# Induced attention and gated network on one core: one planner setting for all stretches, an earlier second softmax, reciprocals by a bit guess and three Newton steps

## The chip, the cores and the metric

The kernel runs on one core of one Trainium2 chip. The metric is the device time of one launch in microseconds (us); three runs of the kernel before gave 713.29, 713.41 and 719.63 us, median 713.41. Engines are named as in the profile: PE (matrix products), PEld (its weight loads), DVE (VectorE), ACT (ScalarE), POOL (GpSimd) and SP (the queue that issues most transfers).

## The reference

```python
def mab(q, kv):                      # x: 4 x 12416 x 128, inducing: 32 x 128
    s = scale * (q @ kv.transpose(0, 2, 1))
    s = s - s.max(-1, keepdims=True)
    a = np.exp(s)
    a /= a.sum(-1, keepdims=True) + 1e-09
    return a @ kv
h = mab(I, x)                        # first softmax: 32 rows over 12416 tokens
y = mab(x, h)                        # second softmax: each token over 32 rows
gate = 1.0 / (1.0 + np.exp(-(y @ w_gate)))          # 128 -> 1536
out = gate * (y @ w_val) @ w_out                    # 1536 -> 128
```

## The kernel before

Each of the four batches has 97 groups of 128 tokens. The second softmax is not applied to h: the kernel multiplies h by the two weight matrices once per batch (`hw`, two parts of 12 x 128 columns), so that a token's 32 attention weights, spread four times over the 128 partitions and transposed by a DMA (`a2r`), give gate and value directly. The main loop works on 97 **blocks**, 96 of 512 tokens of one batch and a last one of four times 128 tokens, one piece from each batch. Each block has 12 **chunks** j of 128 hidden columns. For a chunk PE fills 512 columns of gate and of value in PSUM (`emit_fill`, L1172 to L1190), ACT takes tanh(gate / 2) into `t16` (`emit_gate`, L1192), DVE makes u = (t + 1) * value in one SCALAR_TENSOR_TENSOR (`emit_product`, L1206), and PE multiplies the four quarters of u with `wo16` and adds them up in the block's output bank (`emit_out`, L1222 to L1238: four **output products** to a chunk). After 12 chunks ACT moves the bank out, times 0.5 (`emit_evict`, L1248), and SP stores it.

Chunks go through in **steps** of two and one in turn: PSUM has one bank pair (two-chunk) and one bank (one-chunk) for gate and the same for value. So the value fill of a step must wait until the product of the step of its own size ahead of it has read the bank, and the gate fill until that step's tanh has. There are three `t16` buffers and `UBUFS = 5` u buffers for each size: a product writes the buffer of the fifth product of its size ahead of it, and has to wait until that one's output products are done.

An **aside** is a chunk that DVE doesn't work on. PE fills its gate and value in a side bank (L1557), ACT takes the tanh (L1567), POOL adds 1 (L1571), ACT copies the value out of PSUM (L1575), and POOL multiplies (L1578). Its four output products belong to the same block as the others, and a block's bank is moved out after its last output product, asides included.

Beside this loop run, for later blocks: the second softmax in groups of 16 x 128 tokens (`op_stage2`: scores on PE, copy by ACT L474, row maximum by a tree on POOL L484 to L492, exponential on ACT L502, sums by a tree on POOL L510, reciprocals on POOL `s2_inverse_pool` L532, spread on POOL L562, transposing DMA on SP L573), and the first softmax of the next batch (`op_stage1`; its group sums are 28 to 32 small PE matmuls into `hp_ps`, L356).

The order of all this on every engine is made when the kernel is built, by a planner in the kernel: it keeps a time for each engine and, for each operation, a cost and a time to its result, and takes at each point what is ready. `TIMES` says from which place (batch, chunk of four blocks) an operation of the softmaxes may start: "late" gives the starts of the second softmax's groups 2 to 5. `SETTINGS` are thresholds of the planner, one row for each stretch of eight blocks; rows only name what differs from the row before. Among them: `most` asides in a block, `lead` (an aside is begun only where the next product lies at least so many planned ns behind ACT), `eager` (how far an eviction may push a tanh), `guard` (PE work in the last 3413 planned ns below which PE gets a matmul with zeros, a **pulse**, L1745). Engines run their queues in the planned order; the planned times themselves are not used on the chip, where semaphores decide.

## Time and profile before

| | |
|---|---|
| median of 3 runs | 713.41 us |
| the profiled execution's own time | 713.61 us |
| its span, first to last instruction | 711.7 us |
| busy in the span: PE, DVE, ACT, POOL | 695.2, 696.7, 676.5, 477.6 us |
| first product begins, last one ends | 30.46, 707.13 us |
| products on DVE, asides on POOL | 762 steps (1143 chunks), 21 |

A group's row of the profile has the line of the kernel, engine, operation, the tile written and the tiles read, the shapes and how often; then busy time of the group in us and mean ns of one instruction; then idle time ahead of it and what ended it. Durations of neighbouring instructions on one engine overlap a little, so that the busy time of a group (without the overlap) is less than count times mean. A row of a timeline has the start and how long it took in us, and neighbours of one kind are merged (x3). The row of a window has, for each engine, the busy us and the instructions, then the granted clock of TensorE.

### The profile page before, as it was taken

What the parts mean: (1) busy time and instruction counts of PE and PEld (TensorE: products, weight loads), DVE (VectorE), ACT (ScalarE), POOL (GpSimd) and SP (SyncE); (2) the same over time, 40 slices, a digit from 0 to 9 for tenths busy, and PEclk for the clock granted to TensorE, in tenths of its full rate; (3) what the DMA queues carried; (4) which work ended last, traced back from release to release, by engine and by line L of the source; (5) the groups of instructions that cost most, each with busy time, mean ns of one, the idle gap of its engine ahead of it and who ended that gap; (6) DMA issues with size and microseconds to landing.
All of it is one profiled execution on the core that took longest, in us unless ns stands there. A gap on an engine that the chain in (4) does not pass through costs nothing.

```text
span 711.7 us, 21558 instructions
## 1 busy us (share of the span) xinstructions
PE 695.2 (98%) x8449; PEld 409.0 (57%) x8449; DVE 696.7 (98%) x864; ACT 676.5 (95%) x1035; POOL 477.6 (67%) x743
## 2 busy tenths in 40 slices
PE   7999999999999999999999999999999999999997
PEld 4455555655555555655555555565565565565555
DVE  5899999999999999999999999999999999999997
ACT  4699999999999999999999999999999999999996
POOL 3587577868776874889865785678755688774221
PEclk9999999999999999999999999999999999999999
DMA  9795795324369534243448532302022022122011
GB/s 208 115 190 120 132 161 113 86 81 97 100 131 166 117 69 113 68 105 63 100 86 156 94 92 61 89 33 74 34 76 76 31 76 60 47 76 76 32 46 46
DMA packets 118181, 65.76 MB, mean 92 GB/s; under 512 B 101408, under 2 KB 102208, under 8 KB 118080
## 3 DMA queue, kind: packets, MB, share of 16 engines
q1 hardware_dynamic: 112176, 50.90, 31.2%
q0 software_dynamic: 5584, 13.34, 11.3%
q8 instruction: 66, 1.08, 0.6%
q14 instruction: 35, 0.29, 0.1%
q10 hardware_dynamic: 320, 0.15, 0.1%
HBM read 27.80 MB, written 25.43 MB: 75 GB/s over the span
## 4 chain that ended last, share of the span: by engine, by line
PE 79%; DVE 8%; ACT 7%; issue 2%; DMA 2%; POOL 1%; DVEq 0%; ACTq 0%; POOLq 0%
PE acc_ps L1231 39%; PE v_ps L1180 30%; DVE u L1206 7%; ACT t L1194 6%; PE g_ps L1180 5%; DMA xn<-in_x_dram 2%; PE s_ps L431 2%; PE hp_ps L356 1%; PE s_ps L296 1%; POOL xT L562 0%; ACT o L1248 0%; PE xt_ps L617 0%; PE side_g_ps L1557 0%; POOL hpart L660 0%; PE hw_ps L397 0%
## 5 line engine op out<-in xcount | busy, mean ns | idle before, releaser
L1206 DVE SCALAR_TENSOR_TENSOR u<-t,v_ps 128x1024 f16<-128x1024 f16 x763 | 664.8, 944 | 0.7 <-PE acc_ps L1231 0.3
L1194 ACT ACTIVATE t<-g_ps 128x1024 f16<-128x1024 f32 x762 | 583.2, 831 | 14.2 <-ACT t L1194 5.7
L1231 PE MATMUL acc_ps<-wo,u 128*128 128x128 f16 x4572 | 388.0, 221 | 1.9 <-ACT o L1248 1.6
L1231 PEld LDWEIGHTS <-u 128*128 128x128 f16 x4572 | 262.5, 98 | 165.3 <-issue 162.8
L1180 PE MATMUL v_ps<-a2r,hwt 32*128 32x512 f16 (+1 forms) x1167 | 291.8, 375 | 4.5 <-DVE u L1206 1.1
L1180 PE MATMUL g_ps<-a2r,hwt 32*128 32x512 f16 (+1 forms) x1167 | 290.4, 374 | 0.0
L1180 PEld LDWEIGHTS <-hwt 32*128 32x128 f16 x2358 | 106.0, 91 | 94.3 <-issue 10.7
L562 POOL TENSOR_TENSOR a2n<-e,rs 128x2048 f16<-128x2048 f16 (+1 forms) x23 | 83.9, 3648 | 1.8
L535 POOL TENSOR_TENSOR near<-sme,minus 128x16 f32<-128x16 f32 (+1 forms) x22 | 65.2, 2963 | 1.8
L1248 ACT ACTIVATE o<-acc_ps 128x512 f32<-128x512 f32 x96 | 58.4, 609 | 0.0
L486 POOL TENSOR_SCALAR rise<-rise 128x256 f32<-128x256 f32 (+6 forms) x110 | 51.0, 463 | 9.5
L1571 POOL TENSOR_SCALAR side_t<-side_t 128x512 f32<-128x512 f16 x21 | 31.4, 1496 | 30.3 <-ACT side_t L1567 30.2
L1578 POOL TENSOR_TENSOR side_t<-side_t,side_v 128x512 f16<-128x512 f32 x21 | 26.7, 1270 | 30.9 <-ACT side_v L1575 27.0
L484 POOL TENSOR_TENSOR rise<-sc 128x256 f32<-128x256 f32 (+1 forms) x22 | 16.2, 737 | 43.7 <-ACT sc L474 43.4
L510 POOL TENSOR_TENSOR sum<-e 128x256 f32<-128x256 f16 (+1 forms) x23 | 15.4, 670 | 44.3 <-ACT e L502 42.1
L510 POOL TENSOR_TENSOR sum<-sum 128x128 f32<-128x128 f32 (+3 forms) x92 | 28.3, 307 | 7.1
L488 POOL TENSOR_TENSOR top<-top,rise 128x128 f32<-128x128 f32 (+3 forms) x88 | 28.3, 322 | 6.8
L484 POOL TENSOR_TENSOR rise<-top 128x128 f32<-128x128 f32 (+3 forms) x88 | 27.2, 309 | 6.5
L492 POOL TENSOR_TENSOR sc<-sc,top 128x512 f32<-128x512 f32 (+1 forms) x22 | 23.9, 1085 | 1.7
L321 ACT ACTIVATE a1T<-s_ps,nm 128x512 f16<-128x512 f32 (+1 forms) x26 | 16.8, 646 | 3.3 <-DVE nm L308 3.2
L431 PEld LDWEIGHTS <-xT 128*128 128x128 f16 x388 | 14.2, 96 | 6.9 <-issue 6.4
L431 PE MATMUL s_ps<-hT,xT 128*128 128x32 f16 x388 | 17.9, 177 | 0.1
(157 smaller groups left out, 333.1 us busy)
## 6 DMA issues: line engine op xcount, KB each, us to landing
out_dram<-o SPq DMA_DIRECT2D x96, 256.0 KB, 2.1
xn<-in_x_dram POOLq DMA_DIRECT2D x18, 512.0 KB, 6.4
xn<-in_x_dram POOLq DMA_DIRECT2D x3, 544.0 KB, 6.2
xn<-in_x_dram POOLq DMA_DIRECT2D x3, 256.0 KB, 12.8
xn<-in_x_dram SPq DMA_DIRECT2D x1, 576.0 KB, 4.7
xn<-in_x_dram SPq DMA_DIRECT2D x1, 512.0 KB, 3.8
a2r<-a2n SPq DMA_TRANSPOSE x27, 4.3
wg<-in_moe_w_gate_dram POOLq DMA_DIRECT2D x1, 384.0 KB, 11.6
```

The source lines that it names most:

```text
L431: nc.tensor.matmul(s2[:, j, :], xT[b][:, c + j, :], hT16[b][:], start=(j == 0), stop=whole and j == j1 - 1, skip_group_check=True,)
L484: nc.gpsimd.tensor_tensor(out=r, in0=far, in1=near, op=ALU.subtract)
L486: nc.gpsimd.tensor_scalar_max(out=r, in0=r, scalar1=0.0)
L510: nc.gpsimd.tensor_tensor(out=d[:, 0:n, :], in0=src[:, :, 0:w], in1=src[:, :, w : 2 * w], op=ALU.add)
L535: nc.gpsimd.tensor_tensor(out=near[:, 0:n], in0=sme[:, 0:n], in1=minus1[:, 0:n], op=ALU.pow)
L562: eng.tensor_tensor(out=a2n[:, 0:n, :, :], in0=e.unsqueeze(2).to_broadcast((P, n, 4, m)), in1=rs.unsqueeze(2).unsqueeze(3).to_broadcast((P ...
L1180: nc.tensor.matmul(pt[:, k, col : col + nb * P], hw[b][r : r + 32, j // 2, :], a2r[r : r + 32, o : o + nb, :].rearrange("p j t -> p (j t)" ...
L1194: st["tanh"] = nc.scalar.activation(out=st["t"][:], in_=st["g"][:], func=AF.Tanh, scale=0.5)
L1206: u = nc.vector.scalar_tensor_tensor(out=st["u"][:, :, c:e], in0=st["t"][:, :, c:e], scalar=1.0, in1=st["v"][:, :, c:e], op0=ALU.add, op1= ...
L1231: nc.tensor.matmul(accs[i][(q // 2) % len(accs[i])][:, q, :], u[:, ts(q, P)], wo16[:, item["j"], :], start=begins, stop=last, skip_group_c ...
L1248: nc.scalar.mul(out=o32[:], in_=accs.pop(i)[0][:], mul=0.5)
L1571: nc.gpsimd.tensor_scalar_add(out=st["t1"][:], in0=st["t"][:], scalar1=1.0)
```

## The change

- One row of settings for all stretches, with `lead` 1900 (1500 or 1900 before), `most` 6 everywhere, and three new thresholds. `gap` is so large that it does nothing. With `rush`, an eviction may push a tanh by up to 2500 planned ns once 44 output products are queued. `ripe` halves the wait after which an aside's fill may go out of turn (4000 to 2000).
- The starts of the second softmax's groups move up by 0 to 6 places.
- Reciprocals: one power on POOL and a Newton step (4 instructions) become a bit guess by integer arithmetic and three Newton steps (10 instructions).
- The PE matmuls of a first softmax's group sum go out in one piece, not in two.
- In the last block, value and gate fills of a step are interleaved where both are ready.
- Pulses may begin earlier; the aside's sum has one buffer, not two; the zeros are set by DVE at the start. `HALVES` is off, `TBUFS` and `DEEP` keep the old numbers.

```diff
-    dict(most=6, warm=1500, margin=300, loose=150, lead=1500, calm=26, outq=40, quiet=1,
...
+    dict(most=6, warm=1500, margin=300, loose=150, lead=1900, calm=26, outq=40, quiet=1,
+        slack=90, guard=1800, hold=22, eager=300, keep=0, pace=9999, soft=80, push=36,
+        patience=6000, hurry=100, window=320, age=3500, ahead=21, ripe=2000, gap=1000000,
+        rush=44),
+    dict(),
...
-        "late": {2: 5, 3: 20, 4: 36, 5: (52, 56)},
+        "late": {2: 5, 3: 19, 4: 34, 5: (46, 50)},
...
-        nc.gpsimd.tensor_tensor(
-            out=near[:, 0:n], in0=sme[:, 0:n], in1=minus1[:, 0:n], op=ALU.pow
+        nc.gpsimd.tensor_scalar(
+            out=near[:, 0:n].bitcast(I32),
+            in0=sme[:, 0:n].bitcast(I32),
+            scalar1=-1.0,
+            scalar2=float(0x7EF31200),
+            op0=ALU.mult,
+            op1=ALU.add,
         )
         yield
         off = s2p.tile([P, GC + NLO], F32, tag="off")
...
+        for k in range(3):
+            nc.gpsimd.tensor_tensor(
+                out=off[:, 0:n], in0=sme[:, 0:n], in1=near[:, 0:n], op=ALU.mult
+            )
+            yield
+            nc.gpsimd.tensor_scalar(
+                out=off[:, 0:n],
+                in0=off[:, 0:n],
+                scalar1=-1.0,
+                scalar2=2.0,
+                op0=ALU.mult,
+                op1=ALU.add,
+            )
+            yield
+            nc.gpsimd.tensor_tensor(
+                out=(near if k < 2 else rs)[:, 0:n], in0=near[:, 0:n], in1=off[:, 0:n], op=ALU.mult
+            )
+            yield
...
-        p0 = add("PE", 160, 300, lambda: part(0, 2), [c, loaded[b, s]], sum_at, COL, opens=True, work=107)
...
-        p1 = add("PE", 160, 300, lambda: part(2, 4), [p0], None, COL, work=107) if full else p0
+        cost = 310 if full else 160
+        p1 = add("PE", cost, cost + 140, lambda: part(0, 4), [c, loaded[b, s]], sum_at, COL, opens=True, work=cost * 0.7)
...
-            elif tau - f.born > 4000:
+            elif tau - f.born > knob["ripe"]:
...
-                go = spare >= (-knob["eager"] if x.rank < 0 else -knob["hurry"] if tau - x.seen > knob["age"] else 0)
+                go = spare >= (-knob["eager"] if x.rank < 0 and queued() < knob["rush"] else -2500 if x.rank < 0 else -knob["hurry"] if tau - x.seen > knob["age"] else 0)
...
-        if i < NB - 1 and todo[i] < NJ and tau > 4000 and recent(tau) < knob["guard"]:
+        if i < NB - 1 and todo[i] < NJ and tau > 1000 and recent(tau) < knob["guard"] * min(1, tau / 3413):
```

The plan that comes out differs from the first dozens of steps on. It has 17 asides, where it had 21, so that DVE makes 1147 chunks instead of 1143, in 764 steps instead of 762; 11 pulses instead of 3; and 122 more instructions on POOL. Two places are shown, without the weight loads (LDWEIGHTS) that stand ahead of each matmul. Lines of the changed kernel are its own: its output products are L1244, its fills L1203, its pulses L1788, its tanh L1209, its asides' value copy L1614.

**First place, PE at the 73rd product.** Steps are counted from 1. A name with v_ps is a value fill, g_ps a gate fill, and an acc_ps row one of the output products that read the u (or side_t, for an aside) named last. Before, product 73 writes u16_2097, in the buffer of u16_1903; its value fill is v_ps_2086, that of product 74 v_ps_2106.

```order
L1231 MATMUL acc_ps_1840<-wo16_108,u16_1903 128x128
L1231 MATMUL acc_ps_1960<-wo16_108,u16_1903 128x128
...
L1180 MATMUL v_ps_2086<-a2r_1453,hwt_563 128x512
L1180 MATMUL g_ps_2089<-a2r_1453,hwt_563 128x512
...
L1231 MATMUL acc_ps_1960<-wo16_108,u16_2049 128x128
L1180 MATMUL v_ps_2106<-a2r_1453,hwt_563 128x512
```

In the changed kernel product 73 writes u16_2078, in the buffer of u16_1864; its value fill is v_ps_2010, that of product 74 v_ps_2054. The aside side_t_1921 is the last piece of its block (acc_ps_1802).

```order
L1244 MATMUL acc_ps_1802<-wo16_108,u16_1864 128x128
L1788 MATMUL acc_ps_1802<-wo16_108,zero16_132 128x512
...
L1203 MATMUL v_ps_2010<-a2r_1429,hwt_563 128x512
L1203 MATMUL g_ps_2013<-a2r_1429,hwt_563 128x512
L360 MATMUL hp_ps_2019<-xn_1_91,a1_1378 32x128
...
L1203 MATMUL v_ps_2054<-a2r_1429,hwt_563 128x512
L1203 MATMUL g_ps_2056<-a2r_1429,hwt_563 128x512
L1788 MATMUL acc_ps_1802<-wo16_108,zero16_132 128x512
L1244 MATMUL acc_ps_1802<-wo16_108,side_t_1921 128x128
L1244 MATMUL acc_ps_2067<-wo16_108,u16_1864 128x128
L1244 MATMUL acc_ps_2067<-wo16_108,u16_1886 128x128
```

What moved: the last output products that read the old contents of product 73's buffer stood far ahead of the value fill of product 74; now four of the eight stand behind it, behind two pulses and behind the aside.

**The same place on ACT.** Before, t16_2063 is the tanh of product 73; the asides' work lies around it.

```order
L1194 ACTIVATE t16_2044<-g_ps_2032 128x512
L321 ACTIVATE a1T_2054<-s1_ps_2024,nm1_1_143 32x128
L1194 ACTIVATE t16_2063<-g_ps_2051 128x1024
L1567 ACTIVATE side_t_2080<-side_g_ps_2070 128x512
L1194 ACTIVATE t16_2092<-g_ps_2068 128x512
```

In the changed kernel t16_1996 is the tanh of product 73, and side_v_2006 the value of the aside.

```order
L1209 ACTIVATE t16_1984<-g_ps_1969 128x512
L1209 ACTIVATE t16_1996<-g_ps_1989 128x1024
L1614 COPY side_v_2006<-side_v_ps_1948 128x512
L1209 ACTIVATE t16_2016<-g_ps_2000 128x512
L1209 ACTIVATE t16_2052<-g_ps_2013 128x1024
L375 COPY hst_1_146<-hp_ps_2019 128x129
```

What moved: the value copy of the aside that the block waits for comes right behind the tanh of product 73.

**Second place, PE at the end.** Before, the last two steps had two chunks and one chunk (u16_15602 and u16_15623), and every fill stood ahead of the last output products.

```order
L1180 MATMUL v_ps_15590<-a2r_3668,hwt_563 128x128
...
L1180 MATMUL v_ps_15606<-a2r_3668,hwt_563 128x128
...
L1231 MATMUL acc_ps_15556<-wo16_108,u16_15602 128x128
L1231 MATMUL acc_ps_15557<-wo16_108,u16_15602 128x128
...
L1231 MATMUL acc_ps_15556<-wo16_108,u16_15623 128x128
```

In the changed kernel the last two steps both have two chunks (u16_15709 from v_ps_15688, u16_15744 from v_ps_15732).

```order
L1203 MATMUL v_ps_15688<-a2r_3406,hwt_563 128x128
L1203 MATMUL g_ps_15689<-a2r_3406,hwt_563 128x128
...
L1244 MATMUL acc_ps_15673<-wo16_108,u16_15686 128x128
L1244 MATMUL acc_ps_15674<-wo16_108,u16_15686 128x128
L1203 MATMUL v_ps_15732<-a2r_3406,hwt_563 128x128
...
L1244 MATMUL acc_ps_15673<-wo16_108,u16_15709 128x128
...
L1244 MATMUL acc_ps_15673<-wo16_108,u16_15744 128x128
```

What moved: the last value fill goes into the same two-chunk bank pair as the one ahead of it, so it stands behind that step's product, and only 16 output products are left behind it.

More of the change, by code (lines that the diff above doesn't have):

```diff
@@ L63 @@
 UBUFS = 5
+HALVES = False
+TBUFS = 3
+DEEP = 2
 DRAG = (8, 20, 40)
@@ L1130, in spread @@
                 it = s2_inverse_pool(n, st["sme"])
-                for _ in range(4):
+                for _ in range(10):
                     next(it)
@@ L1404, in need, with split, run_fill @@
         return r
-    def run_fill(kind, st, start):
-        o = Op("PE", FILL, FILL_LAG, lambda: emit_fill(st, kind.lower()), kind=ROW, work=53 * st["cnt"])
+    def split(st):
+        return st["chunks"][0][0] == NB - 1
+    def run_fill(kind, st, start, mate=None):
+        mine = (st, kind.lower())
+        if mate is None:
+            o = Op("PE", FILL, FILL_LAG, lambda: emit_fill(*o.fills), kind=ROW, work=53 * st["cnt"])
+            o.fills = [mine]
+        else:
+            o = Op("PE", FILL, FILL_LAG, lambda: None, kind=ROW, work=53 * st["cnt"])
+            mate.fills.append(mine)
         run(o, start)
@@ L1513, with near @@
     rooms = {"t": [], "t1": [], "v": []}
+    def near(h, tau):
+        return all(d.done + reach(d, h.eng) <= tau + knob["gap"] for d in h.deps)
     def maybe_aside(tau):
@@ L1530, in maybe_aside @@
             if h.start is None and h.after is not None and h.after <= soon:
-                if all(d.start is not None for d in h.deps):
+                if all(d.start is not None for d in h.deps) and near(h, tau):
                     return
-            if h.start is None and h.after is None and all(d.start is not None for d in h.deps):
+            if h.start is None and h.after is None and all(d.start is not None for d in h.deps) and near(h, tau):
                 return
@@ L1692, in do_act @@
         go = False
+        near = r is not None and r <= tau + 200
         if x is not None:
```

124 lines of the change are left out of this document (64 added, 60 removed).

## The prediction

> **What bounds the kernel now.** I read the busy line first, then the table of windows for the main loop, then the groups of DVE with their shapes kept apart.
>
> ```profile
> span 711.7 us, 21558 instructions
> PE 695.2 (98%) x8449; PEld 409.0 (57%) x8449; DVE 696.7 (98%) x864; ACT 676.5 (95%) x1035; POOL 477.6 (67%) x743
> L1206 DVE SCALAR_TENSOR_TENSOR u<-t,v_ps 128x1024 f16<-128x1024 f16 x763 | 664.8, 944 | 0.7 <-PE acc_ps L1231 0.3
> ```
>
> Three engines look full in shares, so the shares don't decide. The window from the first product to the last does:
>
> ```profile
> core 0: us, PE busy (x) PEld busy (x) DVE busy (x) ACT busy (x) POOL busy (x), PEclk, DMA share, GB/s
> 30.46:707.00 676.54, 670.08 (x8115) 394.82 (x8115) 675.76 (x799) 660.71 (x999) 464.17 (x710) 1.00 0.42 89
> ```
>
> DVE is busy 675.76 of 676.54 us and idle for 0.78; ACT has 15.8 us free, POOL 212. PE's 670.08 is no bound, since its rows overlap. So the main loop lasts as long as DVE's queue of products, and a change is worth what it takes from that queue or puts between its members. Products also wait a little without showing as idle. A stretch near the start, where DVE ran 19 products in a row (10 steps of two chunks, 9 of one, 29 chunks), gives the pace without waits:
>
> ```profile
> 40.01 16.78 DVE L1206 SCALAR_TENSOR_TENSOR u<-t,v_ps 128x1024 f16<-128x1024 f16 x19
> ```
>
> That is 16.78 / 29 = 0.579 us for a chunk. Over all 1143 chunks it is 664.8 / 1143 = 0.582. The difference, 0.003 x 1143 = 3.4 us, with the 0.8 idle makes 4.2 us: all that better feeding could ever give back.
>
> **The change part by part.** *Fewer asides.* The new plan makes 17 asides, not 21, and DVE takes the four chunks: 4 x 0.582 = **+2.3 us**, all on the bounding engine. What it frees elsewhere (for each aside the four rows below) lies on engines with room.
>
> ```profile
> L1567 ACT ACTIVATE side_t<-side_g_ps 128x512 f16<-128x512 f32 x21 | 12.7, 606 | 0.0
> L1575 ACT COPY side_v<-side_v_ps 128x512 f32<-128x512 f32 x21 | 12.5, 596 | 0.0
> L1571 POOL TENSOR_SCALAR side_t<-side_t 128x512 f32<-128x512 f16 x21 | 31.4, 1496 | 30.3 <-ACT side_t L1567 30.2
> L1578 POOL TENSOR_TENSOR side_t<-side_t,side_v 128x512 f16<-128x512 f32 x21 | 26.7, 1270 | 30.9 <-ACT side_v L1575 27.0 <-issue 3.9
> ```
>
> *The late aside.* The order on PE has one new knot. Product 73 must wait for the eight output products of the u buffer's old contents. In the new plan four of them stand behind the value fill of product 74, which waits for the end of product 72, then behind two pulses, then behind the aside, whose value copy stands on ACT behind the tanh of product 73. Nothing hides this: DVE has no other work queued than products, in order. Before, these output products stood far ahead of that fill, and I find no other place in the new order where a buffer's release stands behind a fill that waits for the product just before. To price it I take a stretch of the old trace with the same chain, tanh, value copy, POOL multiply:
>
> ```profile
> 444.18 2.93 DVE L1206 SCALAR_TENSOR_TENSOR u<-t,v_ps 128x1024 f16<-128x1024 f16 x3
> 444.53 1.04 ACT L1194 ACTIVATE t<-g_ps 128x1024 f16<-128x1024 f32 x1
> 444.71 0.72 PE L1231 MATMUL acc_ps<-wo,u 128*128 128x128 f16 x10
> 445.43 0.62 ACT L1575 COPY side_v<-side_v_ps 128x512 f32<-128x512 f32 x1
> 446.13 1.27 POOL L1578 TENSOR_TENSOR side_t<-side_t,side_v 128x512 f16<-128x512 f32 x1 [0.26 <-ACT side_v L1575]
> 446.55 0.39 PE L1180 MATMUL v_ps<-a2r,hwt 32*128 32x512 f16 x1
> 446.91 0.34 PE L1231 MATMUL acc_ps<-wo,u 128*128 128x128 f16 x3
> L1206 DVE SCALAR_TENSOR_TENSOR u<-t,v_ps 128x1024 f16<-128x1024 f16 x381 | 462.0, 1213 | 0.6 <-PE acc_ps L1231 0.3 <-PE v_ps L1180 0.2
> ```
>
> The three products end at 447.11; the third, a two-chunk one of 1.21, began at 445.90, and its tanh had ended at 445.57. The copy behind that tanh ended at 446.05, POOL took over 0.08 later (a handover, which I use for all of them) and ended at 447.40, 1.50 after that product began. In the new plan the same product must wait on: handover 0.08, eight output products (ten took 0.72 with a last one of 0.22, so 0.056 apart: 7 x 0.056 + 0.22 = 0.61), handover 0.08. Product 73 begins 1.50 + 0.77 = **2.3 us** late. From below PE alone gives a bound: handover 0.08, fill to output products 0.36 (446.55 to 446.91), two pulses, 0.61 and 0.08.
>
> ```profile
> 10.77 0.59 PE L607 MATMUL xt_ps<-xT 128*128 128x512 f16 x2
> ```
>
> Two matmuls of 512 columns took 0.59 where one takes 0.38, so they are 0.21 apart, two pulses cost 0.42, and the bound is 1.55. From above POOL may be late: its queue ahead of the multiply is a softmax group's sums, reciprocals, a load's issue, the spread, the aside's sum and another issue.
>
> ```profile
> L510 POOL TENSOR_TENSOR sum<-e 128x256 f32<-128x256 f16 (+1 forms) x23 | 15.4, 670 | 44.3 <-ACT e L502 42.1
> L510 POOL TENSOR_TENSOR sum<-sum 128x128 f32<-128x128 f32 (+3 forms) x92 | 28.3, 307 | 7.1
> L517 POOL TENSOR_SCALAR sme<-sum 128x16 f32<-128x16 f32 x19 | 4.9, 259 | 1.7
> L535 POOL TENSOR_TENSOR near<-sme,minus 128x16 f32<-128x16 f32 x18 | 52.8, 2934 | 1.5
> L540 POOL TENSOR_TENSOR off<-sme,near 128x16 f32<-128x16 f32 x18 | 4.0, 223 | 1.2
> L544 POOL TENSOR_SCALAR off<-off 128x16 f32<-128x16 f32 x18 | 3.7, 204 | 1.6
> L553 POOL TENSOR_TENSOR rs<-near,off 128x16 f32<-128x16 f32 x18 | 4.0, 221 | 1.5
> L562 POOL TENSOR_TENSOR a2n<-e,rs 128x2048 f16<-128x2048 f16 (+1 forms) x23 | 83.9, 3648 | 1.8
> L138 POOL DMA_DIRECT2D xn<-in_x_dram x26 | 15.7, 613 | 0.4 <-issue 0.3
> ```
>
> Sums 0.67 + 4 x 0.31 + 0.26 = 2.2; reciprocals 0.20 + 3 x 0.65 = 2.1; spread 3.6; sum 1.5; two issues 1.2: 10.6 us. The exponential that starts it stands on ACT behind the tanh of product 59, and from there to the end of product 72 are 14 products of 16.78 / 19 = 0.88, or 12.4 us. POOL is ready 1.7 us before product 72 ends, 1.9 before the multiply can start (446.13 against 445.90). I take 2.3.
>
> *The end.* Two two-chunk steps now follow each other, and the last value fill waits for the product ahead of it.
>
> ```profile
> 704.79 0.41 PE L1180 MATMUL v_ps<-a2r,hwt 32*128 32x128 f16 x8
> 705.78 1.90 PE L1231 MATMUL acc_ps<-wo,u 128*128 128x128 f16 x31
> 693.11 14.02 DVE L1206 SCALAR_TENSOR_TENSOR u<-t,v_ps 128x1024 f16<-128x1024 f16 x17
> ```
>
> Handover, such a fill of eight, handover: 0.57 us in which DVE waits. Against it, before DVE ended at 707.13 and PE, with 31 output products queued, at 707.68, 0.55 later; with two left it is 0.08 + 0.06 + 0.22 = 0.36. Net **+0.4 us**, with bounds of 0 and +0.6.
>
> *Reciprocals.* One power of 2.93 and three small ones (0.65) become ten small ones, 2.1: POOL is freed of 1.4 us in each of 22 groups. The integer guess has no row; the small operation and the power bound it (0.20 to 2.93), so the group is between 1.4 shorter and 1.3 longer. POOL's 212 free us cover it; without that cover it would count only in a chain that something waits for, as in the late aside.
>
> *The second softmax sooner.* All its instructions move, scores on PE, copy and exponential on ACT, the chains on POOL, and the transposing transfer on SP, past stores and other transposes there. The count is the same. No product waits for `a2r` in the old trace, so an earlier one gives nothing; it costs nothing as long as ACT's 15.8 and POOL's 212 free us cover it, and if they don't, the tanh is what comes late.
>
> *The rest.* The sum in one piece keeps its matmuls and spares a change between kinds of matmul on PE; the interleaved fills lie where DVE was full (below, 7.00 of 7.00); zeros set by DVE come before its first product. All at 0.
>
> ```profile
> 700.00:707.00 7.00, 6.52 (x131) 5.03 (x125) 7.00 (x10) 5.12 (x8) 0.00 (x0) 1.00 0.10 40
> ```
>
> **The sum:** 2.3 + 2.3 + 0.4 = +5.0 us, if products elsewhere wait as little as before. The profiled execution took 713.6, so 718.6; the median of the runs is 0.2 lower, **718.4 us**.
>
> **The rivals.** *A, the aside is in time:* ACT and POOL run further ahead here than at 444 us, and product 73 doesn't wait. That is 718.4 - 2.3 = 716.1. Against it, the bound of 1.55 comes from PE's order alone.
>
> *B, better feeding pays (not slower):* the uniform plan, with four asides fewer on ACT, takes away every hidden wait, and the late aside too: 716.1 - 4.2 = 711.9. It decides if the products' mean falls to 0.579 a chunk. Against it, the waits are small and scattered.
>
> *C, POOL is late too:* the integer guess is as slow as the power (+2.7) and the two issues take 1 us more. The 1.9 of margin is gone and the multiply comes 1.8 later: 720.2. It decides from 1.9 us of delay on.
>
> *D, ACT loses its lead (slower by over 1%):* the single setting lets side work pass closer to the tanh. The tanh at 444.53 was done 0.33 us before its product began, and a value copy takes 0.60. If each of the 96 evictions and 17 asides costs a product 0.04 us, 4.5 us: 722.9. It decides from 0.02 on each. For it speaks that ACT is 98% busy in the loop; against it, that it loses work.
>
> *E, the clock drops* at the late aside, where PE runs short of work. At half speed the 32 queued output products would take 32 x 0.056 = 1.8 us longer: 720.2. The rows show a granted clock of 1.00 in the whole loop. [...]
>
> **How the numbers follow.** Forecast 0.49, A 0.14, B 0.10, C 0.10, D 0.12, E 0.05. A measurement of this kernel can tell about 1% from no change, so faster means under 706.3 and slower over 720.5. Nothing above reaches 706.3, since B takes all waits away: 0.01 is left for what I don't see. Slower is D, nearly half of C, some of E and the forecast's upper end: 0.18. The range goes from 713.8, which leaves B out, to 721.6, which leaves D out: those two are the 2 in 10.
>
> **What would show it.** Right: DVE again busy nearly all of the loop with products of 0.58 us a chunk; one idle of about 2.3 us ahead of a product at about 94 us (30.5 + 72 x 0.88), ended by output products, with the value copy right behind a tanh and the POOL multiply next to each other before it; a second one of about 0.6 us before the last product; reciprocals of some 0.2 us each on POOL. Wrong: no idle at 94 us (A), a mean under 0.58 us a chunk (B), the multiply held up by the spread or a load's issue (C), idle spread over the loop and ended by ACT (D), a clock under 1 in a window at 90 to 100 us (E).

## The result and the profile after

The changed kernel takes 717.99 us (median of 19 executions, 716.60 to 722.32), the kernel before, run beside it, 713.30 us (19 executions). The ratio is 1.0062, with a 95% interval of 1.0048 to 1.0076: slower by 0.6%, 4.7 us. The prediction said 718.4.

The profiled execution took 717.50 us, 3.89 more than the one of before (713.61). From its page and its table of windows, first product to last:

```profile
span 715.7 us, 21707 instructions
PE 696.1 (97%) x8457; PEld 409.3 (57%) x8457; DVE 697.8 (97%) x866; ACT 676.3 (94%) x1029; POOL 434.2 (61%) x866
L1221 DVE SCALAR_TENSOR_TENSOR u<-t,v_ps 128x1024 f16<-128x1024 f16 x765 | 665.9, 946 | 3.7 <-PE acc_ps L1244 2.2
30.50:711.20 680.70, 671.05 (x8127) 395.27 (x8126) 676.98 (x801) 660.44 (x993) 420.62 (x833) 1.00 0.41 89
```

The loop is still as long as DVE's queue: 676.98 of 680.70 us. It grew by 680.70 - 676.67 = 4.03 us (30.46 to 707.13 before). DVE's idle time in it went from 0.8 to 3.7 us, and the products' own time from 664.8 to only 665.9, though there are four chunks more. Two places hold most of the idle time. The first, in the timeline:

```profile
93.10 2.42 DVE L1221 SCALAR_TENSOR_TENSOR u<-t,v_ps 128x512 f16<-128x512 f16 x3
94.34 0.61 POOL L142 DMA_DIRECT2D xn<-in_x_dram  x1
95.03 0.58 ACT L1614 COPY side_v<-side_v_ps 128x512 f32<-128x512 f32 x1
95.77 1.26 POOL L1617 TENSOR_TENSOR side_t<-side_t,side_v 128x512 f16<-128x512 f32 x1 [0.81 <-ACT side_v L1614]
96.08 0.39 PE L1203 MATMUL v_ps<-a2r,hwt 32*128 32x512 f16 x1
96.47 0.61 PE L1788 MATMUL acc_ps<-wo,zero 128*128 128x512 f16 x2
97.08 0.23 PEld L1244 LDWEIGHTS <-side_t 128*128 128x128 f16 x4 [0.50 <-POOL side_t L1617]
97.08 0.40 PE L1244 MATMUL acc_ps<-wo,side_t 128*128 128x128 f16 x4
97.32 1.28 PE L1244 MATMUL acc_ps<-wo,u 128*128 128x128 f16 x20
97.74 1.22 DVE L1221 SCALAR_TENSOR_TENSOR u<-t,v_ps 128x1024 f16<-128x1024 f16 x1 [2.22 <-PE acc_ps L1244]
```

Read it from the last row back. DVE idled 2.22 us until the output products that free its u buffer. They stand behind the aside's four on PE, those behind POOL's multiply, and that behind ACT's copy, which ended at 95.61. PE's two pulses are not what ended the wait: the weight load behind them stood 0.50 us for POOL's multiply, which ended at 97.03. It was close, though: the second pulse ended at 97.08. The second place is the end, where the last product waits 0.59 us for its value fill:

```profile
709.38 0.40 PE L1203 MATMUL v_ps<-a2r,hwt 32*128 32x128 f16 x8
709.92 1.29 DVE L1221 SCALAR_TENSOR_TENSOR u<-t,v_ps 128x768 f16<-128x768 f16 x2 [0.59 <-PE v_ps L1203]
710.93 0.79 PE L1244 MATMUL acc_ps<-wo,u 128*128 128x128 f16 x8 [0.59 <-DVE u L1221]
```

The new reciprocals, by their groups: the integer guess took 0.204 us, the other small operations of the group 0.204 to 0.222.

```profile
L539 POOL TENSOR_SCALAR near<-sme 128x16 int32<-128x16 int32 x18 | 3.7, 204 | 1.5
L550 POOL TENSOR_TENSOR off<-sme,near 128x16 f32<-128x16 f32 x54 | 12.0, 222 | 4.1
L554 POOL TENSOR_SCALAR off<-off 128x16 f32<-128x16 f32 x54 | 11.0, 204 | 4.7
L563 POOL TENSOR_TENSOR near<-near,off 128x16 f32<-128x16 f32 x36 | 7.9, 221 | 3.0
```

The profiled execution had a mean granted clock of 0.999. Nine of the 19 executions had 0.997 or more and took 716.60 to 718.16 us (median 716.93); the other ten had 0.986 to 0.994 and took 717.80 to 722.32. The kernel before was at 0.999 or 1.0 in all 7 executions beside experiments 1 to 4, and at 0.993 to 0.995 in 3 of the 23 beside experiments 5 to 7 (717.48 to 721.06 us). It had none under 0.997 in the 7 beside 8 to 10, and 0.995 in 4 of 18 beside 11 and 12 (716.84 to 718.64 us). It loses clock too, but less often. One more execution of the kernel before, beside 11 and 12, was slow (792.92 us at 0.656) and is left out. So the median of the change holds some clock loss that its profile doesn't show; experiment 12 does.

### The profile page after: what moved, and what is told of

It is laid out like the page before. It is cut to its first block, busy times and chain, and to the rows that moved or that the text cites. A ratio compares the mean times of both kernels' runs of the same rounds, so it can differ in the third digit from the quotient of the medians.

```text
span 715.7 us, 21707 instructions
## 1 busy us (share of the span) xinstructions
PE 696.1 (97%) x8457; PEld 409.3 (57%) x8457; DVE 697.8 (97%) x866; ACT 676.3 (94%) x1029; POOL 434.2 (61%) x866
## 3 DMA queue, kind: packets, MB, share of 16 engines
q0 software_dynamic: 5584, 13.34, 11.3%
## 4 chain that ended last, share of the span: by engine, by line
PE 74%; DVE 6%; ACT 5%; issue 2%; DMA 1%; DVEq 0%; ACTq 0%
PE acc_ps L1244 37%; PE v_ps L1203 29%; DVE u L1221 5%; PE g_ps L1203 5%; ACT t L1209 5%; PE s_ps L435 1%; PE hp_ps L360 1%; DMA a<-a1T 1%; DVE nm L312 0%; PE s_ps L300 0%; PE acc_ps L1788 0%; ACT o L1269 0%; ACT a1T L325 0%; PE hw_ps L401 0%; PE side_g_ps L1596 0%
## 5 line engine op out<-in xcount | busy, mean ns | idle before, releaser
L1221 DVE SCALAR_TENSOR_TENSOR u<-t,v_ps 128x1024 f16<-128x1024 f16 x765 | 665.9, 946 | 3.7 <-PE acc_ps L1244 2.2
L1209 ACT ACTIVATE t<-g_ps 128x1024 f16<-128x1024 f32 x764 | 585.7, 829 | 17.9 <-ACT t L1209 7.9
L1244 PE MATMUL acc_ps<-wo,u 128*128 128x128 f16 x4588 | 387.3, 221 | 1.5 <-DVE u L1221 0.6
L1244 PEld LDWEIGHTS <-u 128*128 128x128 f16 x4588 | 262.9, 98 | 165.8 <-issue 163.4
L1203 PE MATMUL v_ps<-a2r,hwt 32*128 32x512 f16 (+1 forms) x1171 | 292.6, 375 | 7.6 <-DVE u L1221 3.5
L1203 PE MATMUL g_ps<-a2r,hwt 32*128 32x512 f16 (+1 forms) x1171 | 291.1, 374 | 0.2
L1203 PEld LDWEIGHTS <-hwt 32*128 32x128 f16 x2366 | 107.2, 91 | 100.0 <-issue 16.8
L1617 POOL TENSOR_TENSOR side_t<-side_t,side_v 128x512 f16<-128x512 f32 x17 | 21.5, 1267 | 41.4 <-ACT side_v L1614 33.9
L1610 POOL TENSOR_SCALAR side_t<-side_t 128x512 f32<-128x512 f16 x17 | 25.4, 1492 | 33.9 <-ACT side_t L1606 32.3
L550 POOL TENSOR_TENSOR off<-sme,near 128x16 f32<-128x16 f32 (+1 forms) x66 | 14.7, 222 | 5.1
```

Of the source, the lines that this page charges most:

```text
L1203: nc.tensor.matmul(*row[n], start=True, stop=True)
L1209: st["tanh"] = nc.scalar.activation(out=st["t"][:], in_=st["g"][:], func=AF.Tanh, scale=0.5)
L1221: u = nc.vector.scalar_tensor_tensor(out=st["u"][:, :, c:e], in0=st["t"][:, :, c:e], scalar=1.0, in1=st["v"][:, :, c:e], op0=ALU.add, op1= ...
L1244: nc.tensor.matmul(accs[i][(q // 2) % len(accs[i])][:, q, :], u[:, ts(q, P)], wo16[:, item["j"], :], start=begins, stop=last, skip_group_c ...
L1610: nc.gpsimd.tensor_scalar_add(out=st["t1"][:], in0=st["t"][:], scalar1=1.0)
```

## The experiments

**1. A sixth u buffer**, order unchanged.

```diff
-    up = ctx.enter_context(tc.tile_pool(name="up", bufs=UBUFS))
+    up = ctx.enter_context(tc.tile_pool(name="up", bufs=UBUFS + 1))
```

> The changed kernel in its own order, with six u buffers of each size instead of five, so that product 73 writes a buffer that nobody reads any more. Theory 1 (the block waits for its late aside, and PE, which works in order, holds everything behind it): product 73 starts at once, but the value fill of product 75 stands behind the aside and 36 output products on PE, so about 2.4 us of idle show ahead of product 75 instead, ended by a value fill and not by output products; the time stays within 0.4 us of the changed kernel's 718.0. Theory 2 (the reuse of the u buffer is the cause by itself): the idle is gone and the time falls by 2.3 us, to about 715.7.

Measured: 717.14 us (4 executions), ratio 1.0058 [1.0043, 1.0073]. The idle time moved two products on:

```profile
98.93 4.68 DVE L1221 SCALAR_TENSOR_TENSOR u<-t,v_ps 128x1024 f16<-128x1024 f16 x5 [2.02 <-PE g_ps L1203]
```

Product 73 now began 0.14 us behind its pace and product 75 waited 2.02, for a gate fill. The buffer only chose who pays: PE took its queue in order (in the first profile the aside's output products begin at 97.08 us and the fills of product 75, next in the queue behind them and the other output products, at 99.01 and 99.02), and what stands behind the aside comes late.

**2. No pulses in block 7**, so none between the fill and the aside's output products.

```diff
-                    o = Op("PE", n / 2.4 + 3, 167 + n / 2.4, lambda n=n: emit_pulse(i, n))
+                    o = Op("PE", n / 2.4 + 3, 167 + n / 2.4, lambda n=n: emit_pulse(i, n) if i != 7 else None)
```

> The changed kernel in its own order, without the six pulses of zeros that PE runs in the block that waits for the late aside. Theory 1 (the wait is set by the aside's chain tanh, value copy, POOL multiply): the idle ahead of product 73 stays at 2.2 to 2.3 us. Theory 3 (it is set by PE's own queue: fill, two pulses, eight output products): it falls by the two pulses, 0.4 us, to 1.9. On the clock: if the pulses are what keeps TensorE's clock up here, a granted clock under 1 shows in a window at 90 to 105 us, and the time rises by 1 to 3 us; if not, the time stays at 717 to 718.

Measured: 719.24 us, ratio 1.0080 [1.0063, 1.0096]. Product 73 was as late as with the pulses (2.38 us behind its pace against 2.31). By itself that is no clean comparison, since the output products ran at half clock here, 0.107 us apart where they are 0.056 apart at full clock, and POOL's multiply ended 1.17 us behind product 72 instead of 1.51. What shows that the aside's chain sets the wait in both is the weight load of its output products, which stood 0.49 us for the multiply here and 0.50 with the pulses. And TensorE lost clock in all four executions (0.987 to 0.996, where 10 of 19 had less than 0.997 with the pulses): the profiled one (0.987) had half clock at 86.0 to 92.8 and 96.2 to 103.0 us, and six more products there were 0.2 to 1.4 us late. Four executions alone don't show that the pulses hold the clock; the last section adds to it. In the windows (times of each engine, instructions, then the granted clock):

```profile
87.40:90.80 3.40, 3.40 (x26) 1.57 (x25) 2.60 (x4) 2.92 (x5) 2.97 (x6) 0.50 0.97 151
97.60:101.00 3.40, 3.40 (x44) 2.81 (x36) 1.57 (x2) 2.00 (x4) 1.25 (x2) 0.50 1.05 179
```

**3. The power in the new plan**: the order of the change, with the old reciprocals (a power and one Newton step) in the place of the new.

```diff
-        nc.gpsimd.tensor_scalar(
-            out=near[:, 0:n].bitcast(I32),
...
+        nc.gpsimd.tensor_tensor(
+            out=near[:, 0:n], in0=sme[:, 0:n], in1=minus1[:, 0:n], op=ALU.pow
+        )
```

> The changed kernel in its own order, with only the reciprocals turned back into the power and one Newton step (four POOL instructions instead of ten at the same places). Theory 1 (POOL is off the path): POOL is busy about 31 us more (22 groups of 1.4), the time stays within 0.3 us, and at the late aside POOL's margin of some 0.8 us is used up, so that the multiply comes at most 0.7 us later there (718.0 to 718.7). Rival (the shorter reciprocals are what keeps the small waits of the products down, as less POOL work would if products waited for POOL elsewhere): the time rises by 1 us or more, with idle ahead of products ended by POOL's chains spread over the loop.

Measured: 724.64 us, ratio 1.0166 [1.0151, 1.0181], so 6.7 us over the change as it is, part of it clock: all four executions had 0.985 to 0.993. Of the changed kernel, then of this one, the same place in the timeline:

```profile
149.55 3.83 POOL L572 TENSOR_TENSOR a2n<-e,rs 128x2176 f16<-128x2176 f16 x1
158.90 0.29 POOL L1021 TENSOR_SCALAR e32l<-e,hx 128x32 f32<-128x32 f32 x1
159.81 0.40 PE L1033 MATMUL lh_ps<-e32l,ones 128*128 128x32 f32 x2
```

```profile
147.15 3.10 POOL L541 TENSOR_TENSOR near<-sme,minus 128x17 f32<-128x17 f32 x1
151.24 3.82 POOL L570 TENSOR_TENSOR a2n<-e,rs 128x2176 f16<-128x2176 f16 x1
160.60 0.29 POOL L1019 TENSOR_SCALAR e32l<-e,hx 128x32 f32<-128x32 f32 x1
160.94 0.41 PE L1031 MATMUL lh_ps<-e32l,ones 128*128 128x32 f32 x2 [1.04 <-POOL e32l L1019]
162.90:169.70 6.80, 6.80 (x53) 3.82 (x52) 5.08 (x6) 4.63 (x8) 0.00 (x0) 0.50 0.00 0
```

The power and its spread end 1.7 us later, so POOL's part of the next batch's combine (`e32l`) comes 1.7 later. A matmul that needs it stands in PE's queue and holds it for 1.04 us. PE did 27 matmuls from 159.5 to 162.9 us, where it did 42 in the changed kernel. It ran the next 6.8 us at half clock (0.50, last row, of the windows), and DVE was busy for 5.08 of them, where it was for all of them in the changed kernel. POOL was idle a third of the time, and yet 1.7 us of it counted.

This place makes 3.8 of the 7.4 us by which the loop of the profiled execution is longer. A second one makes 2.3, from 227 to 235 us: the exponential of a softmax group waits for POOL's subtraction `sc` there, 1.34 us where it waited 0.37 in the changed kernel, the tanh behind it on ACT comes late, and one more window at half clock follows (231.2 to 234.6).

```profile
227.74 0.63 ACT L508 ACTIVATE e<-sc 128x512 f16<-128x512 f32 x1 [1.34 <-POOL sc L498]
228.89 0.69 DVE L1219 SCALAR_TENSOR_TENSOR u<-t,v_ps 128x512 f16<-128x512 f16 x1 [0.77 <-ACT t L1207]
```

The rest lies in single waits of up to 0.5 us.

**4. No aside in block 7**, and a plan made for that: 19 asides, 1145 chunks.

```diff
-        if i >= NB - 1 or len(asides[i]) >= knob["most"]:
+        if i >= NB - 1 or i == 7 or len(asides[i]) >= knob["most"]:
```

> The changed kernel with its planner refusing an aside in the eighth block, the late one; the plan behind it comes out anew, with 19 asides (1145 chunks for DVE, 1147 before) and no product whose buffer is freed behind a fill that waits for the product just before it. Theory 1: the idle at 97 us is gone (-2.3), two chunks fewer on DVE (-1.2), the end waits as it does now (two one-chunk steps follow each other): 718.0 - 3.5 = 714.5. Rival D (the uniform setting costs a little everywhere): only the chunks count, 716.8. If the spread of the changed kernel's runs (716.6 to 719.3, with granted clocks of 0.99 to 1.00) comes from the place of the late aside, the runs here all show 0.998 or more and lie within 1 us.

Measured: 716.80 us, ratio 1.0059 [1.0036, 1.0082]; profiled 715.61 against 717.50. No product near 97 us waits. Two chunks less and no late aside should give 3.3 us or more; 1.9 came, since other products of the new plan wait more (0.5 us at 216.6 and at 635.3, and 0.54 twice at the end, where the changed kernel waits 0.59 once). The executions scatter with the clock as before (715.61 at 0.999, 719.51 at 0.990), so its losses aren't tied to that aside alone.

**5. The new reciprocals alone in the kernel before**, with their costs told to the planner.

```diff
-            z = pool_chain(spread, [3010, 300, 290, 300, 3560 * n / 16], [y, a2n_ring[-1] if a2n_ring else None], chain=("spread", b, s))
+            z = pool_chain(spread, [230, *[240, 225, 240] * 3, 3560 * n / 16], [y, a2n_ring[-1] if a2n_ring else None], chain=("spread", b, s))
```

> The kernel before with the new reciprocals alone: the bit guess and three Newton steps, with their short costs told to the planner, and the old times, settings and two-part sums. Its plan keeps 21 asides, 1143 chunks and 762 steps; one aside stands a block later. Theory 1 (short reciprocals gain only where some wait of PE or DVE ends on POOL late in its chain; the old plan was laid out around the power, so that none does): 713.0 us, within 1 us of the kernel before. Theory 2 (a power costs the end time wherever it stands, by what the new plan lost with it, 6.7 us over 18 long reciprocals, 0.37 us each): about 706.5 us, and not above 710.

Measured: 713.26 us (10 executions; before 713.23 in 23), ratio 1.0006 [0.9968, 1.0045].

```profile
PE 695.4 (98%) x8449; PEld 408.7 (57%) x8449; DVE 696.5 (98%) x864; ACT 676.7 (95%) x1035; POOL 445.1 (63%) x875
```

POOL is busy for 32.5 us less (445.1 against 477.6), DVE as long as before. In the old plan (21 asides and 762 steps as before, one aside a block later) the reciprocals are worth nothing; in the new one, whose order was made with their short costs, 6.7 us hang on them, the clock loss included. The price of an operation off the bound isn't a property of the operation: it is that of the place that the order gives it.

**6. More pulses in the change**: 24 where it has 11, all else in the same order.

```diff
-        slack=90, guard=1800, hold=22, eager=300, keep=0, pace=9999, soft=80, push=36,
+        slack=90, guard=2200, hold=22, eager=300, keep=0, pace=9999, soft=80, push=36,
```

> The changed kernel with the planner's guard raised from 1800 to 2200: the same order, 17 asides and 1147 chunks, with 24 pulses of TensorE in place of 11. Theory 1 (the changed kernel's times scatter from 716.6 to 722.3 us because in some executions single stretches of 3.41 us are granted half the clock, and more work for TensorE holds the clock): all executions at a clock of 0.997 or more, 716.5 to 717.3 us, with the median near 717.0 in place of 718.0. Theory 2 (the scatter has nothing to do with how much TensorE does): median near 718.0 with the same scatter, clocks from 0.986 to 1.0. Theory 3 (the added pulses stand in the way of fills): clock held, but 718 us or more.

Measured: 717.33 us, ratio 1.0050 [1.0024, 1.0076]. Eight of 12 executions had a clock of 0.997 or more, where 9 of 19 had it with 11 pulses, and four still had 0.989 to 0.993 (718.34 to 721.94 us). The direction fits; the numbers are too few to call it shown, and these pulses don't end the clock losses.

**7. No asides at all in the kernel before**: 1164 chunks in 776 steps.

```diff
-        if i >= NB - 1 or len(asides[i]) >= knob["most"]:
+        if i >= 0:
```

> The kernel before with no chunk taken aside: all 1164 chunks go through VectorE in 776 steps, 21 chunks more than before. Theory 1 (a chunk more on VectorE costs its product's 0.582 us, and an aside costs nothing besides): 713.0 and 12.2 make 725.2 us, and the four chunks of the change are worth 2.3 us. Theory 2 (the fills, tanh and POOL work of an aside hold up other work, so that a chunk gained is worth a part of that only): 713 to 720 us, 0.33 us a chunk or less. Theory 3 (without asides VectorE has no relief and PE loses its pace): over 728 us.

Measured: 724.49 us, ratio 1.0132 [1.0082, 1.0181].

```profile
29.96:717.81 687.85, 666.20 (x8120) 399.25 (x8119) 685.53 (x813) 656.09 (x971) 407.51 (x668) 1.00 0.41 88
```

That is 11.3 us for 21 chunks. By the loop a chunk costs 0.53 us (687.85 - 676.67 over 21), by DVE's busy time in it 0.47 (685.53 - 675.76 over 21; the rest is idle time, most of it one wait of 1.5 us at 63.5, at half clock). The prediction's 0.582 was the mean with the waits in it. An aside is worth nearly its whole chunk, and four chunks are 1.9 to 2.1 us.

**8, 9, 10. One part of the change undone**, the planner free to make a new order: the old due times (8), the group's sum in two pieces (9), the old settings by stretch (10).

```diff
-        "late": {2: 5, 3: 19, 4: 34, 5: (46, 50)},
+        "late": {2: 5, 3: 20, 4: 36, 5: (52, 56)},
```

```diff
-        p1 = add("PE", cost, cost + 140, lambda: part(0, 4), [c, loaded[b, s]], sum_at, COL, opens=True, work=cost * 0.7)
+        p0 = add("PE", 160, 300, lambda: part(0, 2), [c, loaded[b, s]], sum_at, COL, opens=True, work=107)
...
+        p1 = add("PE", 160, 300, lambda: part(2, 4), [p0], None, COL, work=107) if full else p0
```

```diff
-    dict(),
-    dict(),
...
+    dict(slack=90, guard=1500, eager=100, push=36),
+    dict(hold=18),
...
```

> The changed kernel with the old table of due times, so that the second softmax begins as late as before; the rest of the change stays. Its order has 17 asides and 1147 chunks as the changed kernel, and three products, the 73rd, 171st and 349th, whose buffer of u is given back by the output products of the step right before, where the changed kernel has the 73rd alone. Theory 1 (the time goes by chunks on VectorE at 0.58 us and by such products at up to 2.3 us each, whichever part of the change brings them): 717.5 and two more of 1 to 2.3 us make 719.5 to 722.1 us. Theory 2 (begun sooner, the second softmax crowds the other work, and costs a good part of the 4.7 us): 714 to 716.5 us.

> The changed kernel with a group's sum in two pieces of PE work again, as the only part undone. Its order has 16 asides and 1148 chunks, two products (the 73rd and the 679th) whose buffer of u comes free in the step right before, and an end with one chunk in the last step. Theory 1 (chunks at 0.58 us and such products at up to 2.3 us): 717.5, 0.6 for the chunk, 1 to 2.3 for the second such product, 0.4 less at the end, together 718.7 to 720.0 us. Theory 2 (the longer piece of PE work holds up fills, and costs a good part of the 4.7 us): 714 to 716.5 us.

> The changed kernel with the old settings by stretch, and the rest of the change. Its order has 19 asides and 1145 chunks, three products (the 177th, 538th and 629th) whose buffer of u comes free in the step right before, none of them the 73rd, and an end with one chunk in the last step. Theory 1 (chunks at 0.58 us and such products at up to 2.3 us): 717.5 less 1.2 for two chunks, less 2.3 for the 73rd, less 0.4 at the end, and 1 to 2.3 for each of the three, together 716.6 to 720.5 us, by the middle 718.5. Theory 2 (the one setting for all stretches is what costs the time): 713 to 715 us.

Measured, 4 executions each: 723.81 us (8), 720.80 us (9), 723.15 us (10), ratios 1.0173 [1.0130, 1.0215], 1.0103 [1.0088, 1.0118], 1.0137 [1.0100, 1.0173]. No part undone gives anything back; each makes it slower than the whole change. The products that the orders had named do wait, in 8 the 171st and 349th, in 9 the 679th, in 10 the 177th, the 538th and, for 0.69 us at 594.4, the 629th:

```profile
186.53 1.22 DVE L1221 SCALAR_TENSOR_TENSOR u<-t,v_ps 128x1024 f16<-128x1024 f16 x1 [0.98 <-PE acc_ps L1244]
346.49 1.22 DVE L1221 SCALAR_TENSOR_TENSOR u<-t,v_ps 128x1024 f16<-128x1024 f16 x1 [1.05 <-PE acc_ps L1244]
```

```profile
635.41 1.22 DVE L1221 SCALAR_TENSOR_TENSOR u<-t,v_ps 128x1024 f16<-128x1024 f16 x1 [0.69 <-PE acc_ps L1244]
```

```profile
189.58 1.22 DVE L1221 SCALAR_TENSOR_TENSOR u<-t,v_ps 128x1024 f16<-128x1024 f16 x1 [1.20 <-PE acc_ps L1244]
514.75 1.82 DVE L1221 SCALAR_TENSOR_TENSOR u<-t,v_ps 128x512 f16<-128x512 f16 x2 [1.15 <-PE acc_ps L1244]
```

Executions at a clock of 0.999 lie in what was expected from chunks and such products (719.01 for 9, 719.60 for 10). The medians of 9 and 10 lie above it, with the other executions at 0.987 to 0.995; the profiled one of 10 (721.73 us) ran at half clock from 710.3 us on, and two of its last products waited 1.31 and 1.13 us. All of 8 had 0.994 or less, with a stretch at half clock in its profile, and lies above it:

```profile
494.40:504.60 10.20, 10.20 (x70) 4.94 (x68) 8.27 (x10) 8.50 (x12) 6.17 (x6) 0.50 0.36 80
```

**11. The aside's copy four tanh earlier on ACT.**

```diff
+    at = planned.index(order.index(early[0])) + 1
+    planned.remove(order.index(early[1]))
+    planned.insert(at, order.index(early[1]))
```

> The changed kernel with one instruction moved: the value copy of the aside in block 7 stands on ACT four tanh earlier, two behind the tanh of its gate; all else in the same order. Theory 1 (the late aside is a chain from ACT's copy over POOL's multiply to PE's output products, and with the copy early the multiply has to wait only for POOL's own queue, the load's issue that ended at 94.95 us where the multiply began at 95.77): the idle time ahead of the 73rd product falls from 2.3 to about 1.5 us, and the end with it, to 717.2 us. Theory 2 (POOL's queue is the late one and the copy never counted): the idle time stays at 2.3 us. Theory 3 (four tanh each 0.6 us later cost as much as is gained): idle times of 0.3 to 0.6 us ahead of the products before the 73rd, and no gain.

Measured: 718.53 us (10 executions), ratio 1.0076 [1.0040, 1.0113], profiled 717.44 at a clock of 0.998.

```profile
93.83 1.82 DVE L1221 SCALAR_TENSOR_TENSOR u<-t,v_ps 128x1024 f16<-128x1024 f16 x2 [0.40 <-PE g_ps L1203]
94.00 0.61 POOL L142 DMA_DIRECT2D xn<-in_x_dram  x1
94.64 1.29 POOL L1618 TENSOR_TENSOR side_t<-side_t,side_v 128x512 f16<-128x512 f32 x1
96.17 0.60 PE L1791 MATMUL acc_ps<-wo,zero 128*128 128x512 f16 x2
96.62 0.39 PE L1244 MATMUL acc_ps<-wo,side_t 128*128 128x128 f16 x4
97.26 1.82 DVE L1221 SCALAR_TENSOR_TENSOR u<-t,v_ps 128x1024 f16<-128x1024 f16 x2 [1.61 <-PE acc_ps L1244]
```

The multiply now follows the load's issue at once, and the 73rd product idles 1.61 us, near the 1.5 of theory 1. But the multiply isn't what ends that wait any more: it is through at 95.92, and the aside's output products begin at 96.62, right behind the two pulses. What is left is PE's own queue, fill, two pulses and eight output products, which the prediction had put at 1.55 as the bound from below. And the 71st idles 0.40, since the tanh behind the copy came later, and first product to last took 680.83 against 680.70: nothing gained, as theory 3 had it. The copy was one of three things that were late, with POOL's multiply behind it and, next in turn, PE's fill and pulses.

**12. The change again**, for another trace; nothing is edited.

> The changed kernel as it is, for another trace. Theory 1 (in part of the executions single stretches of 3.41 us run at half clock, each right behind one in which PE did little work): if the profiled execution has a clock under 0.997, it shows such stretches near 82 to 103 us, where PE has least to do, and products that wait 0.3 to 0.6 us there; time 718 to 719.5 us. If the clock is 0.998 or more, 716.6 to 717.6 us and the same idle time of 2.3 us. Theory 2 (the time scatters with something else): 718 us or more at a clock of 1.0 in all rows.

Measured: 718.28 us (8 executions; two of them at a clock over 0.997, 716.73 and 717.27). The profiled one took 719.93 at 0.991, 2.43 more than the first; 1.97 of that lie between the first product and the last:

```profile
84.00:87.40 3.40, 3.29 (x22) 1.32 (x22) 3.35 (x5) 3.07 (x5) 2.72 (x11) 1.00 0.99 217
87.40:90.80 3.40, 3.40 (x25) 1.63 (x23) 2.86 (x4) 3.15 (x5) 2.90 (x7) 0.50 0.96 156
90.80:94.20 3.40, 3.40 (x26) 1.55 (x23) 2.82 (x3) 2.27 (x4) 3.40 (x3) 0.50 0.14 29
94.20:97.60 3.40, 3.40 (x16) 0.85 (x13) 2.73 (x4) 2.70 (x5) 0.68 (x3) 0.50 1.11 166
97.60:101.00 3.40, 3.40 (x73) 2.54 (x72) 1.15 (x3) 2.44 (x5) 1.73 (x2) 1.00 1.02 174
```

TensorE fell to half clock from 87.4 to 97.6 us, before the late aside. DVE idled 0.31 to 0.67 us four times there, each time ended by a fill, ahead of the 2.25 us at 99.86; a fill of 512 columns took 0.60 us at half clock in experiment 3 (at 165.5 us) and 0.39 at full clock (at 159.5). Losses of this kind are what the median has on top of the first profile.

## Why the prediction came out, point by point

| step of the prediction | predicted, us | measured, us |
|---|---|---|
| four chunks more on DVE | +2.3 | +1.9 to 2.1, at the price of experiment 7 |
| the late aside | +2.3 | +2.2 of idle time (2.31 behind its pace) |
| the end | +0.4 | +0.6, of which PE's tail gave nothing back |
| products elsewhere wait as before | 0 | -0.7 to -0.9, what is left of the loop's +4.03 |
| around the loop | 0 | -0.1 |
| profiled execution | +5.0 | +3.9 |
| clock in part of the executions | 0 | +0.5, median 717.99 over the profile's 717.50 |

*The bound* was right: the loop is DVE's queue, and what isn't in that queue or between its members didn't count in the sum.

*The chunks and the aside* were right in place and chain, and in size within 0.4 us. Experiments 1, 2 and 11 say more about the aside. The buffer isn't what is short: with one more, product 75 pays in the place of 73, because PE's queue stands. The bound from below, fill and two pulses on PE alone, didn't set the wait of the first profile, but it was near: with the copy early (experiment 11) it did, at 1.61 us against the 1.55 of the prediction. From above, POOL was idle for 0.81 us ahead of the multiply, where the prediction had given it a margin of 1.9.

*The end* took 0.6: the tail of PE behind DVE's end was forecast to shorten by 0.19 and shortened by 0.04 (0.51 against 0.55), since the last output products waited for the second half of the product (0.16 us, in their weight loads at 711.26).

*"If products elsewhere wait as little as before"* was the step that failed in size. Their mean fell from 0.582 to 0.581 us a chunk (664.8 / 1143, 665.9 / 1147), which over 1147 chunks is 1.2 us, under a third of rival B's 4.2: 0.2 to 0.5 of it because a chunk more costs less than the mean, the rest because products waited less. Why the new plan feeds them better was not taken apart.

*"Reciprocals: POOL's 212 free us cover it"* came out at 0 in the sum, and the reason given was wrong. Experiment 5 gives 0 for the old plan. In the new one, experiment 3 shows that POOL's free time covers nothing: with the power, its chain comes 1.7 us later, and PE waits for it. The prediction named the exception, a chain that something waits for, but looked for it only at the late aside; it was the combine at 160 us (3.8 us with the half clock behind it) and an exponential at 227 (2.3 us with the same).

*The second softmax sooner, and the rest, at 0 each:* as parts they can't be priced so. Undone one at a time, each costs 2.8 to 5.8 us more (experiments 8 to 10), because the planner answers with another order. What could be priced were features of the final order: how many chunks, which products wait for what, how the last steps fall.

*The rivals.* A is out (the idle time is there). C is out as put: the guess takes 0.204 us, and POOL's multiply waited for the copy. B came in part, as above. D is out: idle time isn't spread over the loop and ACT ends none of it of any size. E holds for part of the executions: its place was near, its cause not, since the clock falls ahead of the aside (at 87.4 us in experiment 12), and its 1.8 us compares with 2.0 of the loop there. Its half speed is what the runs show: a granted clock of 0.50 in experiments 2 and 12, and in 2 output products 0.107 us apart. So the median, 0.4 from the forecast, has two errors against each other: 1.1 us too much for waits, 0.5 too little for the clock. Against the nine executions at 0.997 or more (median 716.93, 3.6 us over the kernel before) they are 1.4 and 1.1. The chain and the chunks were right; that the total came so close is luck in part.

Open: in the first profile the same stretch near 84 us kept its clock, with nearly as little work on PE (25 matmuls from 84.0 to 87.4 us, 22 in experiment 12). The last section has an estimate, that it goes by where the clock's windows begin; no run was made to show it. Why some executions of the kernel before lose clock, no trace here tells.

## What to carry to other kernels

When a planner or scheduler makes the order, price the order that comes out and not the edits: count what lies on the bounding engine, and look for each point where an in-order queue stands at a result that another engine makes late (here PE's at the aside, 2.22 us of idle time on DVE). Free time on an engine, as a share or a sum, covered nothing by itself here: POOL had 212 us of it before, and in experiment 3 a chain of POOL's that ended 1.7 us later held PE for 1.04. Ask for each chain who stands waiting at its end. A place where the matrix engine got little work cost twice there, 1.04 us of PE's time by its wait and 6.8 us at half clock behind it. In the changed kernel the second cost did not come in every execution: nine of 19 had a clock of 0.997 or more, ten 0.986 to 0.994.

## What was not expected of the hardware

Behind the start of the loop, the granted clock of TensorE is 1.0 or 0.5 in these traces, and its changes lie one or more steps of 3.41 us apart: half clock lasted 6.8 us from 162.9 in experiment 3, 10.2 from 494.4 in experiment 8 and 10.2 from 87.4 in experiment 12, and the one stretch at 1.0 lasts 706.56 us in the profile of before and 709.97 in the first of the change, 3.41 more. I added up what PE streamed in each such window of 3.41 us, in output products (a fill of 512 columns uses 32 of the 128 rows and counts as one, other matmuls by their rows and columns). The loop's median is 37 to a window. A matmul counts in the window in which it starts. In the 14 traces here, 16 windows at half clock stand in the loop, and each follows a window with at most 25. Of 44 windows with at most 25, 16 were followed by half clock and 28 not; of 2730 with more, none. In the kernel before, and in experiment 5, no window has less than 27. PE needn't be idle in a window ahead of half clock: it was busy for 3.29 of 3.40 us at 84.0 us in experiment 12, with 22 matmuls, and the next 10.2 us had 0.50. The count alone doesn't tell which of the 44 windows are followed by half clock.

If a matmul is shared between the windows in which it streams (512 columns in 0.21 us; at half clock I took twice that, an estimate from output products 0.107 us apart in experiment 2 and 0.056 at full clock), the windows at full clock part further: all seven with 22.0 or less were followed by half clock, and of those with more, which begin at 23.4, only one was, with 24.7, near the end of experiment 10. The windows begin elsewhere in the two traces of the changed kernel: in the first profile the one from 82.8 us held 23.4 and the clock stayed; in experiment 12 the one from 84.0 held 21.8 and it fell. Laid at every place along the trace, a window of 3.41 us holds 20.9 at the least in the changed kernel and never under 25.0 in the kernel before; without the pulses of block 7 (experiment 2) 13.5, in part at half clock. So my estimate is that whether an execution of the change loses clock near 84 us goes by where the windows begin. It is read from eight falls and not shown by a run, and it leaves something over: 7 of the 55 executions of the kernel before beside the experiments had 0.993 to 0.995, and none of them was profiled.

An integer TENSOR_SCALAR on POOL over 128x16 took 0.204 us, as the same with floats, where a power took 2.93.
